# Adding the FFN result to the residual: VectorE adds replaced by accumulating transfers in three of four blocks, with a new instruction order

## The chip, the cores and the metric

The kernel runs on one core of one Trainium2 chip. The metric is the time of one execution on the device in microseconds (us). A core has five engines with a queue of instructions each: PE (TensorE, matmuls), ACT (ScalarE), DVE (VectorE), POOL (GpSimd) and SP (SyncE, which here only issues transfers). Each takes its instructions strictly in the order in which they were written, and waits on semaphores for the others. Transfers run on 16 DMA engines. SBUF is the on-chip memory with 128 partitions, PSUM the memory into which TensorE writes.

## What is computed

Two layers stand one behind the other on a sequence of 2048 tokens with 640 features, in bfloat16: a long convolution with gating (its convolution over 2048 tokens is written with an FFT), then a gated FFN with 1728 hidden features. Each has a layer norm ahead of it and a residual around it.

```python
def _A_ref(q, k, v, shift_k, ssm_k, ssm_D):
    ...
        k_shift = k_shift + k_pad[:, t:t + S, :] * shift_k[:, ks - 1 - t][None, None, :]
    kv = k_shift * v
    ...
    y_f = kv_f * kf_f[None, :, :, :]
    y = irfft2(y_f)[:, 0, :S, :]
    y = y + kv * ssm_D[None, None, :]
    return q * y

def _B_ref(x, w_gate, w_up, w_down):
    g = _silu(x @ w_gate)
    u = x @ w_up
    return (g * u) @ w_down

x = A_q
h = x + _A_ref(_layernorm(x), A_k, A_v, A_shift_k, A_ssm_k, A_ssm_D)
h2 = h + _B_ref(_layernorm(h), B_w_gate, B_w_up, B_w_down)
```

The last line is the one that matters here: the FFN result is added to h.

## The kernel before

The 2048 tokens are handled in four blocks (0 to 3) of 512. A block lies in SBUF as 128 partitions with four tokens each; one of the four columns of tokens (j = 0 to 3) is a tile of 128 x 640.

**What a block does.** `xload` brings x into one of two buffers, xh0 (blocks 0 and 2; in lists of the order xh_72) or xh1 (blocks 1 and 3; xh_73). `ln1` takes its mean and variance (L793 and L796 on ACT), the power on POOL (L806) and normalizes (L815). `kv` loads k (kT, transposed on the way) and v (vt) and makes the short convolution. `xfwd` transforms the product: matmuls with a table (L584, in block 2 L622), evacuated by ACT into tiles X and FO. `prod` multiplies spectra on DVE (tiles T and Y, from the filter's spectra C). `inverse` goes back (L832), multiplies (L859), and makes the second layer norm of each column: ACT sums (L870, L872, L876), POOL takes a power (L883), ACT applies it (L886, L888), and SP transposes the result into hnT. The filter's spectra are made once at the start from kc (its four loads are kc_100 to kc_103).

**The FFN of a block** (`ffn`) is 14 gate-and-up tiles: ten matmuls of 128x512 each (L913 gate, L914 up; a 14th of five, L924, holds the rest of both). ACT evacuates each as a SiLU (gu, L936) and a copy (ub, L938, two buffers), and DVE multiplies them (L940). Then come four groups of 26 down matmuls (L956) into PSUM, one for each column j, with a pair (L968) that adds the 14th tile.

**The residual add**, which the change touches, has three forms. Which blocks use which is set by the tuples RD and RA. Before, RA = (0, 1, 2): ACT evacuates a down result into the SBUF buffer dn5 (tile dn, L976) and adds the mean that the first layer norm had taken away; DVE then adds dn to xh (L983). Block 3 has one DVE instruction for both (L986). Behind it SP writes xh to the output (L990).

**What hangs on it.** The x of block 2 is loaded into the buffer of block 0, and that of block 3 into the buffer of block 1. So the load waits for the four output transfers of the block before last, which wait for its four sums. SP takes its queue in order: whatever stands behind an output transfer waits with it.

**PSUM** has four units of 128 x 1024 float32. A gate-and-up tile, a transform tile or a down result takes one, from its first matmul until ACT or DVE has read it. TensorE can be four tiles ahead of ACT, not more.

**The order.** Each instruction (or group) is a task with a number; the table `ORDER` lists for every engine its tasks in the order in which they are written out. The function `schedule` follows the lists, assigns the PSUM units and puts a few filler matmuls (L249) where it reckons with a pause of TensorE; `emit` writes the instructions with their waits.

Of the kernel before, what the change touches and what calls it, by code (L numbers as in the profile page):

```python
# [58 lines left out]
class _Graph:  # L59
# [170 lines left out]
    def emit(self, block):  # L230
# [75 lines left out]

ORDER = {
    "pe": """
# [7 lines left out]
    """,  # L316
    "act": """
# [12 lines left out]
    """,  # L330
    "dve": """
# [10 lines left out]
    """,  # L342
    "pool": """
        5 6 10 11 8 7 9 151 202 195 209 205 216 198 212 219 134 336 135 421 403 394 412 529 610 628 601 619 736 822 813 840
        831
    """,
    "sp": """
# [3 lines left out]
    """,  # L351
}

# [1 line left out]
def bass_sequential_preLN__ssm_conv_h3__swiglu_ffn__prompt_kernel(  # L355
# [38 lines left out]
    with ExitStack() as es:  # L394
# [67 lines left out]
        epc = sb("epc", o + 544, [4], f32)  # L462
        assert o + 576 <= SBB + 16481 - A0, o + 576

        BN, DIRECT, D8, PT, BN2, ST, R4, PAIR, WARM, ACC, EA, KD, RD, LA, RA = (0,), (), (), (0,), (), (0,), ('xf2',), True, 24, (), True, (2, 3), (), (1, 2, 3), (0, 1, 2)
        g = _Graph(nc, es)

        def cpe(n, k):
# [601 lines left out]
```

## Time and profile before

| | us |
|---|---|
| median of 3 runs | 269.81 |
| lowest and highest | 269.46, 269.82 |
| the profiled execution, its own time | 269.68 |
| its span, first to last instruction | 267.8 |
| PE busy in the span | 254.6 |
| ACT busy | 206.8 |
| DVE busy | 201.7 |
| POOL busy | 28.7 |
| granted clock of TensorE | 0.998 |

The page of a profile gives for each engine its busy time, and for each group of instructions (line, engine, operation, tile written <- tiles read, shape, count) busy us, mean ns of one, and how long the engine stood idle just before them, with what ended that wait behind the arrow. Lines of the timeline begin with start and duration in us from the start of the span; in brackets the idle time before and its releaser. A row of the window view gives a stretch and the busy us in it. Matmuls overlap each other, so the duration of one is longer than the distance to the next.

### The profile page before, as it was taken

The page shows a single profiled execution, that of the slowest core. Times are in us where ns is not written, and L with a number is a line of the kernel's source. Part 1 is how long each engine was busy: PE and PEld are TensorE (multiplying, and loading weights), DVE is VectorE, ACT ScalarE, POOL GpSimd, SP SyncE. Part 2 cuts the span into 40 slices and gives each one's busy share as a digit, 9 for nine tenths or more (in the row PEclk, how much of TensorE's full clock was granted, in tenths as well). Part 3 has the DMA queues.
Part 4 walks back from the last instruction along what each step waited for, and adds up shares of the span by engine and source line. Part 5 has one row for each costly group of instructions (what it writes and reads, how often), then busy time and mean ns, then how long its engine had stood idle before and what let it go on. Part 6 is the DMA issues. An engine that isn't in the chain of part 4 may idle for free.

```text
span 267.8 us, 4162 instructions
## 1 busy us (share of the span) xinstructions
PE 254.6 (95%) x1635; PEld 140.1 (52%) x1635; DVE 201.7 (75%) x282; ACT 206.8 (77%) x394; POOL 28.7 (11%) x37
## 2 busy tenths in 40 slices
PE   7899898999999998899899999999999989999995
PEld 5466563445445655444346567544446654444563
DVE  1599999999999998899999999999994000042204
ACT  2799999989887979948989997689799965346400
POOL 1000306011140042000040202000200200000000
PEclk9999999999999999999999999999999999999999
DMA  6999809959755637452000445500000150010004
GB/s 171 345 351 379 316 16 257 143 119 321 137 94 102 103 77 147 98 183 88 2 0 3 100 83 137 174 0 1 0 2 0 19 82 0 0 51 0 0 2 148
DMA packets 43557, 28.47 MB, mean 106 GB/s; under 512 B 32273, under 2 KB 41234, under 8 KB 43538
## 3 DMA queue, kind: packets, MB, share of 16 engines
q1 hardware_dynamic: 41824, 25.58, 35.4%
q0 software_dynamic: 1056, 2.62, 5.4%
q8 instruction: 13, 0.21, 0.3%
q10 hardware_dynamic: 658, 0.01, 0.1%
q14 instruction: 6, 0.05, 0.1%
HBM read 15.69 MB, written 2.62 MB: 68 GB/s over the span
## 4 chain that ended last, share of the span: by engine, by line
PE 41%; ACT 32%; DVE 15%; DMA 5%; SPq 2%; issue 2%; POOL 1%; ACTq 0%; DVEq 0%
PE ps L913 13%; PE ps L914 13%; PE ps L956 8%; PE ps L584 5%; ACT xh L815 4%; ACT ub L938 3%; ACT qo L856 3%; DMA vt<-in_A_v_dram 3%; DVE T L755 3%; ACT qo L872 3%; ACT qo L870 2%; DVE T L761 2%; ACT KT L545 2%; ACT gu L936 2%; DVE gu L940 2%; ACT qo L888 2%
## 5 line engine op out<-in xcount | busy, mean ns | idle before, releaser
L956 PE MATMUL ps<-Wd,gu 128*128 128x384 bf16 (+1 forms) x416 | 59.1, 300 | 0.1
L913 PE MATMUL ps<-hnT,GA 128*128 128x512 bf16 x140 | 53.1, 379 | 1.2 <-DMA hnT<-qo 0.7
L914 PE MATMUL ps<-hnT,UA 128*128 128x512 bf16 x140 | 53.1, 379 | 0.0
L956 PEld LDWEIGHTS ps<-Wd,gu 128*128 128x128 bf16 x416 | 39.9, 98 | 18.1 <-issue 1.6
L913 PE MATMUL ps<-hnT,GB 128*128 128x512 bf16 x120 | 45.5, 379 | 0.7 <-ACT gu L936 0.7
L914 PE MATMUL ps<-hnT,UB 128*128 128x512 bf16 x120 | 45.5, 379 | 0.0
L936 ACT ACTIVATE gu<-ps 128x512 bf16<-128x512 f32 x52 | 30.6, 598 | 17.8 <-PE ps L914 17.6
L938 ACT ACTIVATE ub<-ps 128x512 bf16<-128x512 f32 (+1 forms) x60 | 33.1, 566 | 6.6 <-PE ps L914 3.4
L940 DVE TENSOR_TENSOR gu<-gu,ub 128x512 bf16<-128x512 bf16 x52 | 21.0, 419 | 22.2 <-ACT ub L938 19.6
L755 DVE TENSOR_TENSOR T<-X,C 128x2560 bf16<-128x2560 bf16 x20 | 29.7, 1486 | 0.3
L756 DVE TENSOR_TENSOR T<-X,C 128x2560 bf16<-128x2560 bf16 x20 | 29.7, 1485 | 0.1
L913 PEld LDWEIGHTS ps<-hnT,GA 128*128 128x128 bf16 x140 | 13.7, 98 | 18.1 <-DMA hnT<-qo 1.0
L883 POOL TENSOR_TENSOR mv<-mv,half 128x1 f32<-128x1 f32 x16 | 15.3, 965 | 70.7 <-ACT mv L876 70.7
L584 PE MATMUL ps<-KT,ftab 128*128 128x320 bf16 x128 | 20.5, 301 | 2.0 <-DMA ftab<-cst_ftab 0.9
L914 PEld LDWEIGHTS ps<-hnT,UA 128*128 128x128 bf16 x140 | 13.7, 98 | 15.5
L913 PEld LDWEIGHTS ps<-hnT,GB 128*128 128x128 bf16 x120 | 11.7, 98 | 15.5 <-ACT gu L936 1.7
L761 DVE TENSOR_TENSOR T<-T 128x1280 bf16<-128x1280 bf16 x24 | 19.3, 819 | 0.2
L914 PEld LDWEIGHTS ps<-hnT,UB 128*128 128x128 bf16 x120 | 11.7, 98 | 13.8
L806 POOL TENSOR_TENSOR st<-st,half 128x8 f32<-128x8 f32 x4 | 9.1, 2267 | 91.2 <-ACT st L800 91.2
L771 DVE TENSOR_TENSOR Y<-Y,T 128x2560 bf16<-128x2560 bf16 x12 | 17.8, 1485 | 0.1
L584 PEld LDWEIGHTS ps<-KT,ftab 128*128 128x128 bf16 x128 | 10.3, 97 | 10.7 <-DMA ftab<-cst_ftab 1.4
L815 ACT ACTIVATE xh<-xh,st 128x640 bf16<-128x640 bf16 x16 | 14.5, 933 | 1.6 <-DVE st L808 1.6
(94 smaller groups left out, 372.8 us busy)
## 6 DMA issues: line engine op xcount, KB each, us to landing
kc<-in_A_ssm_k_dram SPq DMA_DIRECT2D x4, 640.0 KB, 9.2
xh<-in_A_q_dram SPq DMA_DIRECT2D x4, 640.0 KB, 4.2
vt<-in_A_v_dram SPq DMA_DIRECT2D x4, 640.0 KB, 6.3
out_dram<-xh SPq DMA_DIRECT2D x16, 160.0 KB, 1.9
Wd<-in_B_w_down_dram SPq DMA_DIRECT2D x1, 1280.0 KB, 6.5
C<-C POOLq DMA_DIRECT2D x1, 1280.0 KB, 13.6
C<-R POOLq DMA_DIRECT2D x1, 1280.0 KB, 9.4
UA<-in_B_w_up_dram SPq DMA_DIRECT2D x1, 1120.0 KB, 9.1
```

Source lines behind the costliest of these rows:

```text
L584: last = e.matmul(pt.f(c, W), ftab[:, cs, j, f * P:(f + 1) * P], src[:, j, c * W:(c + 1) * W], start=(j == par), stop=(j == par + 2))
L755: g.add("dve", nm, lambda e, x=x, k=k, t1=t1: e.tensor_tensor(out=t1, in0=x, in1=k, op=ALU.mult), cdve(2560), r=[x, k], w=[t1])
L756: g.add("dve", nm, lambda e, x=x, k=ksw, t2=t2: e.tensor_tensor(out=t2, in0=x, in1=k, op=ALU.mult), cdve(2560), r=[x, k], w=[t2])
L761: g.add("dve", nm, lambda e, p=p, q=q, d=d, op=op: e.tensor_tensor(out=d, in0=p, in1=q, op=op), cdve(1280), r=[p, q], w=[d])
L771: g.add("dve", nm, lambda e, y=y, z=z: e.tensor_tensor(out=y, in0=y, in1=z, op=ALU.add), cdve(2560), r=[y, z], w=[y])
L815: g.add("act", nm, lambda e, j=j, xj=xj: e.activation(out=xj, in_=xj, func=ACTF.Identity, scale=s[:, 4, j:j + 1], bias=s[:, 5, j:j + 1]), ...
L913: e.matmul(pt.f(0, N), wg[:, c, f0:f0 + P], hnT[:, c, :], start=(c == 0), stop=(c == NC5 - 1))
L914: last = e.matmul(pt.f(1, N), wu[:, c, f0:f0 + P], hnT[:, c, :], start=(c == 0), stop=(c == NC5 - 1))
L936: g.add("act", nm, lambda e, pt=pt, gv=gv, a=ps_g, ts=ts: e.activation(out=gv, in_=pt.f(a[0], N, a[1])[:, ts], func=ACTF.Silu, scale=gain) ...
L938: g.add("act", nm, lambda e, pt=pt, uv=uv, a=ps_u, ts=ts: e.activation(out=uv, in_=pt.f(a[0], N, a[1])[:, ts], func=ACTF.Copy, scale=gain) ...
L940: g.add("dve", nm, lambda e, uv=uv, gv=gv: e.tensor_tensor(out=gv, in0=gv, in1=uv, op=ALU.mult), cdve(n), r=[gv, uv], w=[gv])
L956: last = e.matmul(pt.flat(c1 - c0, P + c0), slots[fb][:, j * P:(j + 1) * P], Wd[:, fb, c0:c1], start=(fb == 0 and not second), stop=(fb == ...
```

## The change

The tuples change places: RD = (0, 1, 2) and RA = (). In blocks 0 to 2 ACT evacuates as before, and the sum is made by a transfer that POOL issues and that adds its source to what its destination holds. The destination is one column of xh (1280 bytes in each partition), the source a column of dn5, which lies there as five runs of 128 elements (256 bytes) in each partition. Twelve DVE additions of 128 x 640 go away, twelve transfers of 160 KB come. Nothing changes in block 3.

```diff
-        BN, ..., RD, LA, RA = (0,), ..., (), (1, 2, 3), (0, 1, 2)
+        BN, ..., RD, LA, RA = (0,), ..., (0, 1, 2), (1, 2, 3), ()
```

The code that the tuples choose between is the same in both:

```python
if i in RD:
    g.add("pool", nm, lambda e, x=x, z=z: e.dma_start(x.rearrange("p (c n) -> p c n", c=NC5), z, accum_op=ALU.add), 1100,
          r=[z, x], w=[x], dma=(1200, 0), lat=1700, lock=False)
else:
    g.add("dve", nm, lambda e, x5=x.rearrange("p (c n) -> p c n", c=NC5), z=z: e.tensor_tensor(out=x5, in0=x5, in1=z, op=ALU.add),
          cdve(D), r=[z, x], w=[x])
```

All five lists of `ORDER` are new, so that nearly every stretch of the program stands in another order. Line numbers of the changed kernel are smaller by one behind the table, which has a line less. One row of each list:

```diff
-        5 6 10 11 8 7 9 151 202 195 209 205 216 198 212 219 134 336 135 421 403 394 412 529 610 628 601 619 736 822 813 840
-        831
+        8 10 6 7 5 11 9 151 202 195 216 205 209 198 219 212 134 336 135 421 403 295 412 394 299 304 308 529 610 601 488 628
+        619 497 501 492 736 822 840 813 831 699 695 708 704
...
-        17 0 18 136 3 19 62 227 57 67 223 224 222 4 310 312 230 311 226 231 225 207 200 214 221 319 323 320 316 315 228 229
+        17 0 18 136 3 62 19 310 67 57 222 4 224 225 312 223 311 207 230 200 221 214 320 316 319 226 315 323 228 229 227 231
```

The first place is POOL's queue from the filter's combination (tile C) to the powers of block 2 (tile mv is the statistics of one column of the second layer norm, st those of the first). Before:

```order
L664 DMA C_51<-R_53 128x4x1280
L883 TENSOR_TENSOR mv_122<-mv_122,half 128x1
L883 TENSOR_TENSOR mv_120<-mv_120,half 128x1
L883 TENSOR_TENSOR mv_119<-mv_119,half 128x1
L883 TENSOR_TENSOR mv_121<-mv_121,half 128x1
L806 TENSOR_TENSOR st_0_117<-st_0_117,half 128x8
```

and in the change:

```order
L663 DMA C_51<-R_53 128x4x1280
L882 TENSOR_TENSOR mv_122<-mv_122,half 128x1
L882 TENSOR_TENSOR mv_120<-mv_120,half 128x1
L979 DMA xh_72<-dn_94 128x5x128
L882 TENSOR_TENSOR mv_121<-mv_121,half 128x1
L882 TENSOR_TENSOR mv_119<-mv_119,half 128x1
L979 DMA xh_72<-dn_94 128x5x128 x3
L805 TENSOR_TENSOR st_0_117<-st_0_117,half 128x8
```

The first transfer of block 0 stands between two powers of block 1, the other three behind the last. Block 1's stand the same way in block 2; block 2's four stand at the end of the queue.

The second place is ACT's queue behind the last evacuation of block 0's FFN (the row just ahead is one L976 before, and two in a row, L975 x2, in the change), up to the first statistics of block 2's x (L793; X_56 and FO are the transform of block 2, gu and ub the first FFN tiles of block 1). Before:

```order
L628 ACTIVATE FO<-ps 128x640 x4
L628 ACTIVATE X_56<-ps 128x640 x2
L938 ACTIVATE ub_79<-ps 128x512
L628 ACTIVATE X_56<-ps 128x640 x2
L936 ACTIVATE gu_81<-ps 128x512
L938 ACTIVATE ub_78<-ps 128x512
L793 ACTIVATE qo_77,st_0_117<-xh_72 128x640
```

and in the change:

```order
L627 ACTIVATE X_56<-ps 128x640
L627 ACTIVATE FO<-ps 128x640
L627 ACTIVATE X_56<-ps 128x640
L627 ACTIVATE FO<-ps 128x640 x2
L627 ACTIVATE X_56<-ps 128x640 x2
L937 ACTIVATE ub_78<-ps 128x512
L937 ACTIVATE ub_79<-ps 128x512
L935 ACTIVATE gu_84<-ps 128x512
L935 ACTIVATE gu_82<-ps 128x512
L935 ACTIVATE gu_81<-ps 128x512
L937 ACTIVATE ub_79<-ps 128x512
L792 ACTIVATE qo_77,st_0_117<-xh_72 128x640
```

L793 (now L792) stands behind six FFN rows from three tiles instead of three rows from two.

The third place is SP's queue at the start of the program. Before:

```order
L481 DMA ftab<-cst_ftab 128x2048
L481 DMA vt<-in_A_v_dram 128x2560
L481 DMA kc_102<-in_A_ssm_k_dram 128x5x512
L481 DMA PK<-in_B_w_up_dram 128x5x64
L481 DMA kc_101<-in_A_ssm_k_dram 128x5x512
L481 DMA kc_103<-in_A_ssm_k_dram 128x5x512
L481 DMA UA<-in_B_w_up_dram 128x5x896
```

and in the change:

```order
L480 DMA ftab<-cst_ftab 128x2048
L480 DMA kc_102<-in_A_ssm_k_dram 128x5x512
L480 DMA vt<-in_A_v_dram 128x2560
L480 DMA xh_73<-in_A_q_dram 128x2560
L480 DMA kc_103<-in_A_ssm_k_dram 128x5x512
L480 DMA kc_101<-in_A_ssm_k_dram 128x5x512
L480 DMA GA<-in_B_w_gate_dram 128x5x896
```

The load of v for block 0 stands behind a load of the filter instead of ahead of it. The rows keep the names of the kernel before in the text that follows.

More of the change, by code (lines that the diff above doesn't have):

```diff
@@ L463, in bass_sequential_preLN__ssm_conv_h3__swiglu_ffn__prompt_kernel @@
         assert o + 576 <= SBB + 16481 - A0, o + 576
-        BN, DIRECT, D8, PT, BN2, ST, R4, PAIR, WARM, ACC, EA, KD, RD, LA, RA = (0,), (), (), (0,), (), (0,), ('xf2',), True, 24, (), True, (2, 3), (), (1, 2, 3), (0, 1, 2)
+        BN, DIRECT, D8, PT, BN2, ST, R4, PAIR, WARM, ACC, EA, KD, RD, LA, RA = (0,), (), (), (0,), (), (0,), ('xf2',), True, 24, (), True, (2, 3), (0, 1, 2), (1, 2, 3), ()
         g = _Graph(nc, es)
```

61 rows, old and new, of the table ORDER are left out of this document.

## The prediction

> **What bounds the kernel now.** I read the page's first part, then the busy time of long stretches, then who waited for whom, and last the timeline at the two places where the residual add meets other work. The page first (engine, busy us, share, instructions):
>
> ```profile
> PE 254.6 (95%) x1635; PEld 140.1 (52%) x1635; DVE 201.7 (75%) x282; ACT 206.8 (77%) x394; POOL 28.7 (11%) x37
> ```
>
> Three stretches of the window view (stretch, its length, then busy us of PE, PEld, DVE, ACT, POOL, the granted clock, the DMA share, GB/s):
>
> ```profile
> 52.11:264.60 212.49, 208.55 (x1237) 111.97 (x1236) 158.77 (x219) 161.97 (x324) 21.16 (x17) 1.00 0.30 71
> 15.00:203.00 188.00, 182.15 (x1161) 98.19 (x1159) 182.86 (x241) 167.33 (x319) 25.69 (x22) 1.00 0.48 119
> 203.00:268.00 65.00, 60.64 (x366) 33.93 (x364) 12.93 (x28) 31.51 (x67) 2.28 (x4) 0.99 0.12 31
> ```
>
> From the first FFN matmul (52.11) to the last down matmul TensorE lacks only 212.49 - 208.55 = 3.9 us, at full clock. That is the most a change behind 52 us can win. VectorE is just as full until 203 us (182.86 of 188) and nearly idle after. So VectorE time counts up to 203 us, but only through TensorE's pauses. Their causes between 52 and 264.6 us (who waited, for whom, us in total, times, longest):
>
> ```profile
> PE ps L968 <- ACT kT L717: 1.1, 1, 1.1
> PE ps L913 <- ACT gu L936: 0.7, 2, 0.6
> PE ps L913 <- DMA hnT<-qo: 0.7, 1, 0.7
> PE ps L913 <- ACT FO L628: 0.5, 1, 0.5
> PE ps L693 <- ACT qo L856: 0.2, 1, 0.2
> PE ps L622 <- ACT FO L628: 0.2, 1, 0.2
> PE ps L968 <- DVE gz L940: 0.2, 1, 0.2
> ```
>
> Together 3.6 us, almost all on ScalarE.
>
> **What is removed.** Twelve VectorE adds and the wait ahead of one of them:
>
> ```profile
> L983 DVE TENSOR_TENSOR xh<-xh,dn 128x640 bf16<-128x640 bf16 x12 | 5.6, 486 | 11.9 <-ACT dn L976 11.8
> 102.53 0.49 DVE L983 TENSOR_TENSOR xh<-xh,dn 128x640 bf16<-128x640 bf16 x1 [1.29 <-ACT dn L976]
> ```
>
> 12 x 0.486 = 5.8 us. Block 2's four fall behind 203 us and are worth nothing. The eight of blocks 0 and 1 are 3.9 us, plus the 1.29 us in which VectorE stood at 102 us: 5.2 us in the stretch where it is full. ScalarE's evacuations (dn) stay as they are.
>
> **What is added.** Twelve accumulating transfers on POOL's queue, 160 KB each, in runs of 256 bytes: 128 x 5 = 640 packets. The trace has the same kind of transfer twice, at 1280 KB in 512 packets of 2560 bytes; the fourth row is the queues part for 77 to 84 us, when only one of them moved, the fifth that for 212 to 219.9 us, when only transposes in 256-byte packets did:
>
> ```profile
> 59.49 1.49 POOL L664 DMA_DIRECT2D C<-C  x1 [12.42 <-DVE C L554]
> 75.14 1.31 POOL L664 DMA_DIRECT2D C<-R  x1
> C<-R POOLq DMA_DIRECT2D x1, 1280.0 KB, 9.4
> q0 software_dynamic: 517, 1.31, 107.3%
> q1 hardware_dynamic: 2688, 0.66, 51.0%
> ```
>
> POOL's issue took 1.4 us for 512 packets, so I put 640 at 1.75 us. An accumulating packet took 1.073 x 16 x 7000 / 517 = 232 ns; a plain one of 256 bytes 0.51 x 16 x 7900 / 2688 = 24 ns. From issue to landing 9.4 us, of which about 7.0 moved data: 2.4 us are fixed. No row has accumulating packets of 256 bytes. By bytes they cost 232 / 10 = 23 ns, per packet 232 ns; each of 16 engines gets 40, so 0.9 to 9.3 us. I take 50 ns, twice the plain packet, hence 2.0 us: the 24 ns row has the same size, and adding reads two operands. Issue to landing is then 2.4 + 0.35 (longer issue) + 2.0 = 4.75 us, between 3.3 and 12.
>
> What lies behind an issue on POOL: one transfer of block 0 stands among the powers of block 1's layer norm, one of block 1 among those of block 2; the others follow the last power. ScalarE's L886 waits for each power. Between the request of the power behind the issue and its L886, ScalarE has two long rows, an L888 and an L870 or an L717 and an L872, some 1.6 us, and the request itself comes about 1.5 us after the issue starts, so 1.75 us and a power of 0.72 are covered. If that cover were gone, ScalarE would stand as it does once now:
>
> ```profile
> L888 ACT ACTIVATE qo<-xh,mv 128x640 bf16<-128x640 bf16 x12 | 10.9, 913 | 0.1
> L872 ACT ACTIVATE qo<-xh,mv 128x640 bf16<-128x640 bf16 x12 | 9.9, 823 | 0.1
> L883 POOL TENSOR_TENSOR mv<-mv,half x16: 544/720/3342, 42.5 to 214.5; 128x1 f32<-128x1 f32 x16
> 100.85 0.29 ACT L886 ACTIVATE mv<-mv 128x1 f32<-128x1 f32 x1 [1.79 <-POOL mv L883]
> ```
>
> 1.79 us there, which became TensorE's 1.1.
>
> **What is late next.** The out transfers wait for the sums, the load of the x that reuses the buffer waits for the out transfers, and ScalarE's L793 stands in order for that x. Blocks 0 to 2, then 1 to 3:
>
> ```profile
> 109.52 0.79 ACT L976 ACTIVATE dn<-ps,st 128x640 bf16<-128x640 f32 x1
> 114.33 1.32 SPq L990 DMA_DIRECT2D out_dram<-xh  x3
> 117.13 0.34 SPq L481 DMA_DIRECT2D xh<-in_A_q_dram  x1
> 112.54 0.38 PE L913 MATMUL ps<-hnT,GA 128*128 128x512 bf16 x1 [0.49 <-ACT FO L628]
> 114.48 0.38 PE L914 MATMUL ps<-hnT,UA 128*128 128x512 bf16 x1
> 117.59 0.60 ACT L936 ACTIVATE gu<-ps 128x512 bf16<-128x512 f32 x1 [0.86 <-PE ps L914]
> 121.09 0.74 ACT L793 ACTIVATE qo<-xh 128x640 bf16<-128x640 bf16 x1 [2.41 <-DMA xh<-in_A_q_dram]
> 128.90 0.39 PE L913 MATMUL ps<-hnT,GB 128*128 128x512 bf16 x1 [0.55 <-ACT gu L936]
> 131.39 0.39 PE L913 MATMUL ps<-hnT,GB 128*128 128x512 bf16 x1 [0.16 <-ACT gu L936]
> 166.07 0.79 ACT L976 ACTIVATE dn<-ps,st 128x640 bf16<-128x640 f32 x1 [0.79 <-PE ps L956]
> 174.55 0.74 ACT L793 ACTIVATE qo<-xh 128x640 bf16<-128x640 bf16 x1 [1.96 <-DMA xh<-in_A_q_dram]
> 120.00:140.00 20.00, 19.29 (x89) 8.42 (x88) 19.80 (x27) 16.98 (x37) 2.96 (x1) 1.00 0.10 40
> 170.00:185.00 15.00, 15.00 (x74) 7.13 (x73) 14.90 (x18) 11.10 (x24) 0.00 (x0) 1.00 0.14 46
> ```
>
> Call D the end of the last dn: 110.31 and 166.86. Now x is used at D + 10.8 and D + 7.7. In the change the third transfer is issued at D - 0.7 (two dn in a row, one lasting 0.79), the fourth at D + 1.05, and lands at D + 5.8. From the last out's issue (114.33 + 2 x 0.44) to the x load 1.9 us, from there to L793 4.0 (121.09 - 117.13): x is there at D + 11.7, that is 122.0 and 178.6: 0.9 and 4.0 us later than now. But L793 has been moved too. In block 2 it now follows the third gate-and-up tile instead of the second. A tile is ten matmuls; the first and the tenth start 1.94 us apart, so a tile takes 2.16 us, and the third ends at 117.59 + 2.16 = 119.75. Four ScalarE rows follow, at about 0.5 us (121.09 - 2.41 - 117.59 = 1.09 for two): L793's turn comes at 121.7. In block 3 it moves from behind the first tile to behind the third. Its turn was at 174.55 - 1.96 = 172.6; two tiles (4.3 us) and two transform pieces of four matmuls come on top (about 0.55 each: from the end of the tenth matmul, 114.86, to 117.59, less a tile): 178. So ScalarE's 2.41 and 1.96 us shrink to a few tenths. TensorE's two pauses at 128.90 and 131.39 hang on the first: -0.7 us. The second has none behind it.
>
> **The order elsewhere.** The pauses between 100 and 113 us (1.1, 0.2 and 0.5) meet a new order in which the pair matmuls stand ahead of the convolution's and one transform piece ahead of the last down group. Their bounds are all gone (-1.8) and a new pause as long as the longest (+1.1); VectorE's freed 5.2 us serve this stretch, so I take -0.4. The remaining 1.1 us (0.2 + 0.2 + 0.7) I leave.
>
> At the front the load of kc_102 (640 KB) now goes ahead of the first vt (a row of the chain of waits, two of the timeline, the GB/s of the 40 slices, one ScalarE stretch):
>
> ```profile
> 7.29 7.57 DMA vt<-in_A_v_dram
> 14.96 1.23 DVE L713 TENSOR_TENSOR vt<-ps,vt 128x1024 bf16<-128x1024 f32 x1 [0.26 <-PE ps L584]
> 16.10 1.01 DVE L786 BATCH_NORM_STATS2 bst<-xh 128x6 f32<-128x320 bf16 x2
> GB/s 171 345 351 379 316 16 257 143 119 321 137 94 102 103 77 147 98 183 88 2 0 3 100 83 137 174 0 1 0 2 0 19 82 0 0 51 0 0 2 148
> 20.00:25.00 5.00, 4.63 (x46) 3.20 (x43) 4.86 (x7) 5.00 (x8) 0.00 (x0) 1.00 1.06 379
> ```
>
> 655 KB at 360 GB/s is 1.8 us that vt and the VectorE chain behind it start later. 1.0 us of statistics is moved ahead of vt, so 0.8 us is left; ScalarE is full there (5.00 of 5) and has other filter rows to do meanwhile. Between 0 and 1.8 I take +0.4.
>
> **Sum.** -0.7 - 0.4 + 0.4 = -0.7 us. The profiled execution took 269.68 us (span 267.8 and 1.9 around it), 0.13 below the median of 269.81. 269.68 - 0.7 = 269.0; on the median 269.1.
>
> [...]
>
> **The rivals.**
>
> *The sums land late (slower).* If a packet of 256 bytes costs near the 232 ns of a large one, landing comes up to 7.3 us later. ScalarE has spare 20 - 16.98 = 3.0 us in 120 to 140 and 15 - 11.1 = 3.9 us in 170 to 185; the wait at L793 decides once it is longer. At half way (+3.65 us) L793 waits 3.9 and 4.2 us: 0.9 + 0.3 lost, and the gain of 0.7 with it: 269.8 + 1.2 = 271.0. At the full 7.3 us it waits 7.6 and 7.9: 4.6 + 4.0 lost, 278.4. Against it: the 24 ns row.
>
> [...]
>
> *The new order costs more than it gives (slower).* Front at its bound, 1.8 instead of 0.4, and pauses at 100 to 113 as now: -0.7 + 1.8 = +1.1: 270.9. For it: ScalarE is full up to 50 us and has no room to make up; against: the moved statistics.
>
> *VectorE's freed time reaches further (faster).* All pauses of 100 to 132 us go (-1.8 - 0.7) and the front costs nothing: 269.81 - 2.5 = 267.3; with the front at 0.4, 267.7. For it: VectorE is full to 203 us.
>
> *It does not show.* The adds are hidden, TensorE pauses elsewhere as long: 269.8.
>
> **How the numbers follow.** Forecast 0.42, its own range 268.2 to 270.1; further reach 0.12, new order 0.26, late landing 0.12, lock 0.04, nothing 0.04. About 0.2% (0.54 us) is what a measurement here can tell from no change, so faster means below 269.27. The forecast's band gives 0.25 faster, 0.15 the same, 0.02 slower; the new order 0.22 slower, 0.04 the same; further reach faster; landing and lock slower. Together 0.37 faster, 0.23 the same, 0.40 slower. The range 267.6 to 271.8 takes in further reach, the new order and half of the late landings.
>
> **What would show it.** Right: no L983 row; 12 more DMA issues on POOL of 1.5 to 2 us; a sum landed about 4.8 us after its issue; L793's waits for x below 1 us; no pause among the gate-and-up matmuls of block 1; first FFN matmul at 52 to 53 us. Wrong: landings over 8 us, L793 waiting over 3 us, powers queued behind an issue with L886 waiting, or a first FFN matmul beyond 53.5 us.

## The result

The change made the kernel slower by 0.32%: 270.47 us median of 20 runs (269.18 to 272.85) against 269.70 for the kernel before beside it (268.38 to 270.05), a ratio of 1.0032 with a 95% interval of 1.0016 to 1.0047. The forecast was 269.1 us, a little faster; the time lies inside the range that went with it (267.6 to 271.8), but on the other side of no change. The profiled execution took 270.92 us with a span of 269.0, against 269.68 and 267.8. Two executions of one kernel below, the old order with transfers, fell into a slower state of the chip; its median below is that of the other four (with all six it is 282.84, which later expectations quote).

### The profile after

The lines that answer to those quoted of before. From the page, the engines (busy us, share, instructions; 16 matmuls are missing from this trace, which has 1637 weight loads), the queue that carries POOL's transfers (packets, MB, share of 16 engines) and the new transfers (number, KB, us from issue to landing):

```profile
PE 253.9 (94%) x1621; PEld 142.2 (53%) x1637; DVE 197.6 (73%) x270; ACT 206.2 (77%) x394; POOL 45.3 (17%) x49
q0 software_dynamic: 8928, 4.59, 15.3%
xh<-dn POOLq DMA_DIRECT2D x12, 160.0 KB, 5.0
```

VectorE lost its 12 additions. The kernel with additions in the same order (below) has in its page:

```profile
q0 software_dynamic: 1056, 2.62, 5.6%
```

The transfers are what was forecast: 8928 - 1056 = 7872 packets took (15.3 - 5.6)% of 16 x 269 us, or 53 ns each (forecast 50), and a sum lands 5.0 us behind its issue (forecast 4.75).

TensorE's pauses behind 52 us, as in the view of who waited for whom (us in total, times, longest):

```profile
PE ps L621 <- DVE vt L725: 1.4, 1, 1.4
PE ps L912 <- ACT gu L935: 1.0, 2, 0.9
PE ps L912 <- ACT ub L937: 0.8, 2, 0.5
PE ps L913 <- ACT FO L596: 0.5, 1, 0.5
PE ps L913 <- DMA hnT<-qo: 0.4, 1, 0.4
PE ps L955 <- ACT kT L716: 0.4, 1, 0.4
PE ps L913 <- ACT FO L627: 0.4, 1, 0.4
PE ps L831 <- DVE IO L553: 0.3, 1, 0.3
```

They add up to 5.3 us where the kernel before had 3.6. Almost none of the old ones is left, and a new set has taken their place. The largest stands in these timeline rows (SP's and POOL's issues, VectorE, TensorE; in brackets the idle time before a row and what ended it):

```profile
96.79 6.79 SPq L485 DMA_TRANSPOSE kvo<-kT  x5
98.98 1.51 POOL L979 DMA_DIRECT2D xh<-dn  x1
104.53 0.96 DVE L725 TENSOR_TENSOR vt<-vt,kvo 128x1536 bf16<-128x1536 bf16 x1 [0.99 <-DMA kvo<-kT]
106.74 0.76 DVE L725 TENSOR_TENSOR vt<-vt,kvo 128x512 bf16<-128x512 bf16 x2 [1.25 <-DMA kvo<-kT]
107.56 0.45 PE L621 MATMUL ps<-vt,ftab 128*128 128x320 bf16 x2 [1.45 <-DVE vt L725]
```

Block 0's first sum is issued at 98.98, in the middle of the five transposes into kvo that block 2's vt waits for. The tile view of kvo in 94 to 109 us gives their time to landing (least, median, most):

```profile
DMA to landing us min/median/max: 2.4/3.9/4.6
```

The same view of the kernel with additions in the same order, where no sum moves, gives

```profile
DMA to landing us min/median/max: 2.4/2.5/2.5
```

So a transpose into kvo with no sum beside it landed in 2.4 to 2.5 us; those next to the sum took up to 4.6. The order places one transform piece of block 2 (L621) ahead of the last down group, so TensorE stands for it. In 102 to 104 us both queues move, each at about 60% of the engines' time (packets, MB, share):

```profile
q1 hardware_dynamic: 821, 0.20, 63.1%
q0 software_dynamic: 328, 0.08, 60.8%
```

One thing more moves there. The first queues row for 104 to 106 us in the change is a single packet of 16 KB on the queue that the view calls "instruction", 4.1% of 16 engines for 2 us, or 1.3 us on one engine; the second is that of the kernel with additions in 103 to 107 us, 1.5 us on one engine; the third is the landing of that kernel's transposes into hnT in 100 to 113 us:

```profile
q8 instruction: 1, 0.02, 4.1%
q8 instruction: 1, 0.02, 2.4%
DMA to landing us min/median/max: 2.6/3.5/5.0
```

The two transposes that go out beside this packet (103.29 and 104.61 us) take 5.0 and 4.3 us though no sum moves; the two behind them take 2.6 and 2.7. In the change the last transpose into kvo, issued at 102.28 behind two that the sum had held up, is still under way when this packet comes, and lands after 4.4 us. With the sum out of the way (first sum late, below) it lands in 2.5, about as the packet comes. So the sum starts the delay, and the packet may add to it; no run removes the packet.

Block 1's sums show the sharing without this packet. The transposes into hnT beside them land, with additions (155 to 172 us) and in the change (160 to 172), in

```profile
DMA to landing us min/median/max: 2.6/2.6/2.6
DMA to landing us min/median/max: 2.6/3.2/4.8
```

### The profile page after: what moved, and what is told of

The parts are those of the page before. It is cut to its first block, busy times and chain, and to the rows that moved or that the text cites. A ratio compares the mean times of both kernels' runs of the same rounds, so it can differ in the third digit from the quotient of the medians.

```text
span 269.0 us, 4149 instructions
## 1 busy us (share of the span) xinstructions
PE 253.9 (94%) x1621; PEld 142.2 (53%) x1637; DVE 197.6 (73%) x270; ACT 206.2 (77%) x394; POOL 45.3 (17%) x49
## 3 DMA queue, kind: packets, MB, share of 16 engines
q0 software_dynamic: 8928, 4.59, 15.3%
## 4 chain that ended last, share of the span: by engine, by line
PE 31%; ACT 27%; DVE 20%; DMA 16%; SPq 3%; issue 1%; POOL 1%; DVEq 0%
PE ps L913 9%; PE ps L912 9%; PE ps L955 5%; DMA xh<-dn 4%; DVE T L755 4%; ACT qo L887 3%; ACT qo L871 3%; DMA xh<-in_A_q_dram 3%; ACT qo L869 3%; DVE T L754 3%; DMA kvo<-kT 3%; PE ps L583 3%; ACT qo L855 2%; DVE Y L760 2%; DVE X L553 2%; ACT ub L937 2%
## 5 line engine op out<-in xcount | busy, mean ns | idle before, releaser
L912 PE MATMUL ps<-hnT,GA 128*128 128x512 bf16 x132 | 50.0, 379 | 0.9 <-ACT gu L935 0.9
L937 ACT ACTIVATE ub<-ps 128x512 bf16<-128x512 f32 (+1 forms) x60 | 33.9, 572 | 18.3 <-PE ps L913 11.1
L912 PE MATMUL ps<-hnT,GB 128*128 128x512 bf16 x117 | 44.4, 379 | 1.0 <-ACT ub L937 0.8
L882 POOL TENSOR_TENSOR mv<-mv,half 128x1 f32<-128x1 f32 x16 | 14.3, 901 | 61.7 <-ACT mv L875 61.7
L979 POOL DMA_DIRECT2D xh<-dn x12 | 18.3, 2049 | 13.8 <-ACT dn L975 13.8
L912 PEld LDWEIGHTS ps<-hnT,GB 128*128 128x128 bf16 x120 | 11.7, 98 | 16.1 <-ACT ub L937 1.6
L805 POOL TENSOR_TENSOR st<-st,half 128x8 f32<-128x8 f32 x4 | 7.6, 1892 | 70.2 <-ACT st L799 70.2
L583 PEld LDWEIGHTS ps<-KT,ftab 128*128 128x128 bf16 x128 | 11.2, 98 | 10.4 <-ACT KT L544 2.0
```

The lines of the kernel that those rows point to most:

```text
L583: last = e.matmul(pt.f(c, W), ftab[:, cs, j, f * P:(f + 1) * P], src[:, j, c * W:(c + 1) * W], start=(j == par), stop=(j == par + 2))
L912: e.matmul(pt.f(0, N), wg[:, c, f0:f0 + P], hnT[:, c, :], start=(c == 0), stop=(c == NC5 - 1))
L937: g.add("act", nm, lambda e, pt=pt, uv=uv, a=ps_u, ts=ts: e.activation(out=uv, in_=pt.f(a[0], N, a[1])[:, ts], func=ACTF.Copy, scale=gain) ...
L979: g.add("pool", nm, lambda e, x=x, z=z: e.dma_start(x.rearrange("p (c n) -> p c n", c=NC5), z, accum_op=ALU.add), 1100, r=[z, x], w=[x], d ...
```

## The experiments

Every kernel was timed beside the kernel before on the same chip. In all of them the planner sets no filler matmuls behind 60 us (before and the change have none there either). Some have a line or more in addition, so line numbers move; the names stay. "Pauses" is the sum of TensorE's pauses behind 52 us that the timeline shows in its profiled execution. It is a rough measure: matmuls of 379 ns start 216 ns apart, so a start that is up to 0.16 us late shows no idle time.

| kernel | median us | before | ratio, 95% interval | pauses us |
|---|---|---|---|---|
| before | 269.70 | | | 3.6 |
| the change | 270.47 | 269.70 | 1.0032 (1.0016 to 1.0047) | 5.3 |
| new order, additions | 270.86 | 270.28 | 1.0027 (1.0009 to 1.0045) | 3.6 |
| old order, transfers | 281.28 | 270.28 | 1.0412 (1.0363 to 1.0460) | 10.9 |
| first sum late | 270.55 | 270.28 | 1.0007 (0.9987 to 1.0027) | 3.6 |
| sums in landing order | 273.87 | 270.28 | 1.0115 (1.0075 to 1.0155) | 5.6 |
| the same, wide runs from elsewhere (FFN result left out) | 268.75 | 269.92 | 0.9954 (0.9933 to 0.9975) | 2.6 |
| old order in the first 86 us | 270.22 | 269.92 | 1.0009 (0.9992 to 1.0026) | 4.2 |
| block 1 on VectorE | 270.00 | 269.92 | 1.0013 (0.9989 to 1.0037) | 2.3 |
| both of these | 270.29 | 269.92 | 1.0016 (1.0000 to 1.0031) | 3.9 |
| **the change, wide runs** | **267.35** | 269.87 | **0.9922 (0.9892 to 0.9953)** | 1.2 |
| landing order, wide runs | 268.38 | 269.87 | 0.9954 (0.9937 to 0.9970) | 2.1 |
| old order, transfers, wide runs | 280.42 | 269.87 | 1.0399 (1.0364 to 1.0435) | 9.9 |
| before, layout alone | 270.19 | 269.87 | 1.0020 (1.0001 to 1.0039) | 4.0 |
| old order, outputs back, wide | 273.59 | 269.93 | 1.0139 (1.0094 to 1.0184) | 7.5 |
| old order, outputs back, small | 279.29 | 269.93 | 1.0344 (1.0272 to 1.0417) | 11.2 |

### The new order with additions

```diff
-RD, LA, RA = (0, 1, 2), (1, 2, 3), ()
+RD, LA, RA = (), (1, 2, 3), (0, 1, 2)
-pool: ... 403 295 412 394 299 304 308 529 ... 601 488 628 619 497 501 492 ... 831 699 695 708 704
+pool: ... 403 412 394 529 ... 601 628 619 ... 831
+dve:  ... 569 295 ... 571 304 ... 572 299 308 ... 773 488 ... 726 497 ... 780 492 ... 778 501 ... 827 695 708 704 699
```

> The changed kernel's order with the twelve sums back on VectorE (each put behind the VectorE instruction that runs when its dn is ready; nothing else is moved; POOL carries powers alone). Theory A, the transfers cost: TensorE's pause of 1.45 us for vt at 107.6 shrinks below 0.5, because nothing shares the queues with the transposes into kvo at 101 to 104 us; x of blocks 2 and 3 is there 3 us earlier or more, L792 no longer waits, and the pause of 0.86 us at 183 goes: 270.9 - 2.0 = 268.9, less what 3.9 us of VectorE take back. Theory B, the new order costs by itself: the pauses at 75 to 85 us (1.0) and at 143 to 172 us (1.25) stay, VectorE's 3.9 us come on top, and the time is that of the changed kernel, 270.5, or above.

Measured 270.86 us, 1.0027: not to be told from the change. Neither theory holds alone. The pause for vt is gone, as A said, and L792 (here L793) no longer waits at 124 us and 0.34 us at 179. But other pauses came, the largest because VectorE is late with the inverse transform's input:

```profile
143.74 2.35 PE L832 MATMUL ps<-IO,itab 128*128 128x320 bf16 x16 [1.07 <-DVE IO L554]
```

The listed pauses add up to 3.6 us, as before, but the span is 269.0 us: 0.3 us of the difference lie ahead of the first FFN matmul (52.45) and 0.9 in late matmul starts that the list does not count. So it seems that in this order taking 12 additions off VectorE does help, and that something in the transfers takes the same amount back; the wide runs below bear it out.

### The old order with transfers

```diff
-RD, LA, RA = (), (1, 2, 3), (0, 1, 2)
+RD, LA, RA = (0, 1, 2), (1, 2, 3), ()
-dve:  (the twelve tasks)
+pool: ... 394 295 412 304 299 308 ... 628 488 601 619 497 492 501 ... 831 708 695 699 704
```

> The order of before with the twelve sums as transfers on POOL (each behind the power that precedes its dn, the late ones behind the last power of the next block; nothing else is moved). Theory A, the transfers cost: the fourth sum of block 0 lands about 5.8 us behind the last dn, x of block 2 is there at 123 us and that of block 3 at 179 instead of 121.1 and 174.5, L793 waits 4.2 and 6.4 us instead of 2.4 and 2.0, and TensorE's pauses behind them grow by 1.8 and about 2: 0.5 to 3 us above before. Theory B, the transfers are innocent and the new order costs: VectorE's 5.2 us come free, 269.7 or up to 0.7 below.

Measured 281.28 us, 11 above before where at most 3 were expected. TensorE stood 8.6 us for hnT, the transposed input of the next FFN. SP and POOL in block 1:

```profile
165.28 5.42 SPq L989 DMA_DIRECT2D out_dram<-xh  x2
166.16 3.04 POOL L979 DMA_DIRECT2D xh<-dn  x2
170.75 4.92 SPq L485 DMA_TRANSPOSE hnT<-qo  x3
```

In the old order two outputs of block 1 stand ahead of three transposes into hnT. With additions these outputs were ready at 162.5; now SP stands at them until the sums have landed, and the transposes go out at 170.75 instead of 163.6; 2.3 us of this are the lateness that the kernel has by then (its transposes into kvo start at 156.93 instead of 154.67).

### The first sum late

```diff
-pool: ... 421 403 295 412 394 299 304 308 ...
+pool: ... 421 403 412 394 295 299 304 308 ...
```

> The changed kernel with one task moved on POOL: the first sum of block 0 goes behind the last two powers of block 1 instead of ahead of them, so it is issued at about 106 us instead of 99. Theory A, this transfer's packets share the queues with the transposes into kvo: these land in about 2.5 to 3.5 us instead of 3.9 to 4.6, VectorE has vt 1 us earlier and TensorE's pause of 1.45 us at 107.6 falls to 0.5 or below: 0.3 to 1.0 us faster than the changed kernel. Theory B, the transposes are late by their place in the queue alone: the pause stays above 1.2 us and the time does not change.

Measured 1.0007, some 0.25% below the change, though the two intervals overlap. The mechanism is as theory A has it: the transposes into kvo land in

```profile
DMA to landing us min/median/max: 2.4/2.5/2.6
```

and the pause for vt is gone. Two others stand in its place. The first sum, issued at 106.97 instead, now meets the last two transposes into hnT, which take 4.7 and 3.7 us to land (with additions 2.7 and 2.6), and TensorE waits 0.71 us for them at 113. At 183 it waits 1.19 for gu, where L792 has waited 1.96 for x.

### Sums in landing order

```diff
-pool: ... 394 299 304 308 ... 619 497 501 492 ...
+pool: ... 394 304 299 308 ... 619 497 492 501 ...
-sp: ... 309 300 296 305 503 ... 502 489 493 498 710 ...
+sp: ... 296 305 300 309 503 ... 489 498 493 502 710 ...
```

> The changed kernel with the sums on POOL, and the output transfers on SP, in the order in which their dn are ready (block 0: third column ahead of the second; the output that lands last goes last, not first; block 1 the same). Theory A, x comes late because sums and outputs stand in the wrong order: x of block 2 is there at about 123 instead of 125.6 us and that of block 3 at 179 instead of 180.9, L792's waits of 1.40 and 1.62 us go, and TensorE's pause of 0.86 us at 183 with them: 0.5 to 0.9 us faster than the changed kernel. Theory B, x does not set the end: the pause at 183 us stays or moves, and the time stays within 0.2 us.

Measured 273.87 us: the order that should have brought x earlier cost 3.4 us more. The third sum of block 1, issued at 165.9 us instead of 168, now moves while the transposes into hnT move. POOL's issues and TensorE's first FFN matmul, from the timeline, and the time to landing of the four transposes, from the tile view of hnT:

```profile
164.44 3.05 POOL L979 DMA_DIRECT2D xh<-dn  x2 [0.77 <-ACT dn L975]
173.15 0.61 PE L912 MATMUL ps<-hnT,GA 128*128 128x512 bf16 x1 [2.83 <-DMA hnT<-qo]
DMA to landing us min/median/max: 2.6/3.8/6.3
```

And x of block 3 did not come earlier: the last two sums of block 1 take 7.2 and 7.6 us to land instead of 4.2 to 5.7, and its load is issued at 177.21 us instead of 176.96. The matmul behind the pause took 0.61 us instead of 0.38 (last section).

### The same with wide runs from elsewhere

```diff
-e.dma_start(x.rearrange("p (c n) -> p c n", c=NC5), z, accum_op=ALU.add)
+e.dma_start(x, GA[:, 0, 0:D], accum_op=ALU.add, max_dma_last_dim=2560)
```

> The kernel of the sums in landing order (273.9 us, TensorE's pause of 2.83 us for hnT at 173), but each sum takes its source from one run of 1280 bytes in each partition instead of five of 256: 128 packets in place of 640. For that it adds a stretch of the gate weights instead of the FFN's result; it still waits for dn, so the instants are those of the transfer. Theory A, the many small packets hold up the transposes into hnT: these land in 2.6 to 3.5 us instead of 4.8 to 6.3, the sums in 3 to 4 instead of 5 to 7.6, the pause falls below 0.7 and the time to 270 to 271. Theory B, the adding of the 160 KB itself holds the queues, whatever the packets: landings and pause stay, 273 to 274.

The source is a stretch of the gate weights, so this kernel leaves the FFN result out; it serves for its time alone. Measured 268.75 us, 5.1 below the kernel with small packets, and 0.46% below before. Transposes, queues, order and bytes are the same; the run length of the source changed, and with it its place, which a later experiment (landing order, wide runs) sets right. Sums land in 3.7 us, the pause for vt is gone and that for hnT is 0.91. Theory A holds, beyond its number.

### Old order in the first 86 us; block 1 on VectorE; both

```diff
 (first sum late, and)
+all five lists: tasks that the planner starts before 86 us in the old kernel, in the old order, then the rest in the new
```

> The kernel with the first sum late (270.55), but every instruction that the planner starts in the first 86 us stands in the order of before; the rest in the new order, with the sums as transfers. Theory A, the new order itself costs in the gate-and-up tiles of block 0 (pauses for ub of 0.26 and 0.34 us at 78 and 85 us, and a first FFN matmul that is no earlier): these pauses go, 0.4 to 0.7 us faster than the first sum late, and so below before. Theory B, ScalarE only hands its backlog on: the same time, 270.3 to 270.8.

```diff
 (first sum late, and)
-RD, LA, RA = (0, 1, 2), (1, 2, 3), ()
+RD, LA, RA = (0, 2), (1, 2, 3), (1,)
-pool: ... 488 ... 497 501 492 ...
+dve:  ... 773 488 ... 726 497 ... 780 492 ... 778 501 ...
```

> The kernel with the first sum late (270.55), but the four sums of block 1 are VectorE additions again, where they stood in the experiment with the new order and additions. Theory A, the transfers of block 1 share the queues with the transposes into hnT of block 2 and make x of block 3 late: the pauses at 170 us (0.23 for hnT) and at 183 us (1.19 for gu) fall to 0.7 in sum, and the time is 0.3 to 0.8 us lower, at that of before or below. Theory B, VectorE's 1.9 us cost as much there: no change.

> Both edits together: the order of before in the first 86 us, then the new order with the first sum late, and block 1's sums on VectorE; blocks 0 and 2 keep transfers. Theory A: the two gains add, 0.7 to 1.5 us below the first sum late, so some 0.5 to 1.2 us below before. Theory B: the time stays at that of before within 0.3 us.

None of the three is told apart from the first sum late (1.0009, 1.0013 and 1.0016 against 1.0007). The pauses for ub at 78 and 85 us did go with the old front, but a wait of 1.10 us for gz at 94 us came where the two orders meet. With block 1 on VectorE the pauses at 170 and 183 us (1.42 in sum) fell to 0.64, as theory A says, and the time did not follow. Its profiled execution had a pause of 3.06 us for kT at 48.8 us that no other shows, so its pauses can't be compared. The two do not add. With small pieces, mixing the forms brought nothing that can be told from noise.

### The change with wide runs

dn5 overlays the last five of the 13 product tiles (gu): the result of a column may only go where that column's own products, already used, have stood. These are five pieces of 256 bytes. If the five tiles lie between each other, the same bytes are one run of 1280. In the cut, `_Five` is a small class that returns the pieces of one such tile; left out are the lines by which ScalarE's SiLU and VectorE's product write a tile in four pieces.

```diff
-dn5 = sb("dn5", o + 8192, [NC5, N])
+dn5 = sb("dn5", o + 8192, [4, NC5, P])
+gu[8:13] = [_Five(dn5, k) for k in range(NC5)]   # tile 8 + k is dn5[:, :, k, :]: four groups of 128, 640 apart
-z = dn5[:, :, P * j:P * j + P]
+z = dn5[:, j]
-e.dma_start(x.rearrange("p (c n) -> p c n", c=NC5), z, accum_op=ALU.add)
+e.dma_start(x, z.rearrange("p c n -> p (c n)"), accum_op=ALU.add, max_dma_last_dim=2560)
```

> The changed kernel in its own order, with the last five product tiles of the FFN laid out so that a column of dn5 is one run: tile 8 + k holds its four groups of 128 columns 640 elements apart, and the five tiles lie between each other. The result of a column then overlays what its own down matmuls have read, as before, but in one run of 1280 bytes: 128 packets for each sum instead of 640. It computes the same. Theory A, the small packets were the cost: a sum lands in 3.7 us instead of 5.0, the transposes into kvo and hnT in 2.6 to 3.2, the pause for vt (1.45 us) falls to 0.3 or less, x comes 1 to 1.5 us earlier, and the time is 1.0 to 1.8 us below the changed kernel, 0.1 to 1.0 below before. Theory B, the new order costs by itself: 0.2% or more above before, as with additions in this order (1.0027).

Measured 267.35 us, 0.9922: 0.8% below before and 3.1 us below the change; theory A expected 1.0 to 1.8. This version beats both. The queue, the sums' landing, all of TensorE's pauses behind 52 us, and POOL's three last issues of block 0:

```profile
q0 software_dynamic: 2784, 4.59, 10.8%
xh<-dn POOLq DMA_DIRECT2D x12, 160.0 KB, 3.4
PE ps L925 <- ACT ub L953: 0.6, 2, 0.3
PE ps L925 <- DMA hnT<-qo: 0.3, 1, 0.3
PE ps L971 <- ACT kT L729: 0.3, 1, 0.3
109.61 2.65 POOL L995 DMA_DIRECT2D xh<-dn  x3 [3.12 <-ACT dn L991]
```

Against the change, in the same order, these have gone: vt 1.45, FO 0.37 and 0.52, IO 0.33, gu 0.86 and 0.19 us; with what came off ub, kT and hnT the list is 4.2 us shorter. The first FFN matmul starts 0.35 us later (52.36), and the spans differ by 3.7 (269.0 and 265.3). That the small pieces cost these pauses is shown; by which way each of them came (transposes, a later x, POOL's issues) is shown for vt alone, by the first sum late. An issue costs POOL 0.88 us instead of 1.52. A packet takes (10.8 - 5.6)% x 16 x 265.3 / 1728 = 128 ns, so the 160 KB of a sum occupy the 16 engines 18 us in all (144 packets) instead of 35 (656). In both, 16 packets of a sum are not pieces of it, which are 128 and 640.

### Landing order, old order and layout alone

```diff
 (the wide layout, in the landing order; in the old order; and in the kernel before with its additions)
```

> The same layout with the sums and outputs in landing order, the kernel that took 273.9 us with small packets. Theory A: as with the stretch of gate weights, 268.8 us, 0.4% below before, and 0.3 us or more faster than the wide layout in the order of the change, since x of block 3 comes 2 us earlier. Theory B, that gain came from the source lying elsewhere, not from its runs: 270 or above.

> The same layout in the order of before, with the twelve sums as transfers, the kernel that took 282.8 us with small packets. Theory A, nearly all of the 12.6 us came from small packets ahead of the transposes into hnT: the waits for hnT (2.3 and 5.7 us) fall below 1 us each, the clock stays at 1.0, and the time comes to 269 to 272 us. Theory B, the old order leaves the transfers no place whatever their packets: 275 us or more.

> The kernel before, with its additions on VectorE and its own order, and only the layout of the last five product tiles and of dn5 changed. Both theories: the layout by itself does nothing, 1.000 within 0.2%; ScalarE's SiLU and VectorE's product on those tiles take 0.60 and 0.43 us as now. Should it be faster by 0.3% or more, the gain of the wide kernels is the layout's and not the packets'.

Landing order: 268.38, as with the source elsewhere, so the gain is the runs'. But its median is 1.0 us above the change's own order, against what I expected (the two intervals just overlap): the third sum still meets the transposes, and TensorE waits 1.06 us for hnT. Layout alone: 1.0020, nothing or a little worse, so the layout does not explain the gain. The old order with wide runs: 280.42, theory B. There the packets alone decide little (0.9 us); hnT is awaited 7.8 us.

### The old order with three outputs moved back

```diff
-sp: ... 397 296 406 415 ... 723 489 498 631 604 622 502 493 ...
+sp: ... 397 406 415 296 ... 723 631 604 622 489 498 502 493 ...
```

> The order of before with the sums as transfers in wide runs (280.4 us), and three outputs moved on SP: the first of block 0 and the first two of block 1 now stand behind the last transpose into hnT of the next block. Theory A, SP's queue held the transposes: those of block 1's sums are issued at about 166 us instead of 172.5, the pause of 3.72 us for hnT falls below 1.5, the clock stays at 1.0 behind it, and the time falls by 5 us or more, to 275 or less. Theory B, the queues are shared whatever SP does: the pause stays above 3 us and the time above 278.

> The same move with small packets (282.8 us before it). Theory A, queue and packets both count: the pause of 5.70 us falls to 2 to 3.5, and the time to 276 to 279, 2 us or more above the wide one. Theory B, the queue alone counts: within 1 us of the wide one.

Measured 273.59 (wide) and 279.29 (small). With small packets the move is worth 2.0 us, and the ranges of the two kernels overlap (277.14 to 281.27 and 280.01 to 283.42); with wide ones it is worth 6.8. Wide packets alone gave 0.9, with the move 5.7: the two together take off 7.7 of the 11.0 us, and neither much alone. Block 1's transposes, in the wide kernel, are issued at once:

```profile
165.18 4.90 SPq L498 DMA_TRANSPOSE hnT<-qo  x3
172.67 0.38 PE L926 MATMUL ps<-hnT,UA 128*128 128x512 bf16 x1 [0.94 <-DMA hnT<-qo]
```

With small packets the pause at that place is 3.62, and the transposes land in up to 6.6 us (wide 4.6). Theory A, queue and packets both, holds in both runs, though the clock did not stay at 1.0 in the wide one (0.51 in 114.6 to 118 us, last section). Where the wide kernel's last 1.4% above before come from stays open; its largest pauses are 2.16 us at 114.7, for ScalarE's evacuation of block 2's transform, and 1.31 at 183.

## Why the prediction was wrong, step by step

**What bounds the kernel**: right in the main. From the change to its version with wide runs the list of TensorE's pauses is 4.2 us shorter and the span 3.7. But the list is not the whole measure, as the new order with additions showed (3.6 us of pauses in spans of 267.8 and 269.0). Of the 3.6 us of before, 2.7 were on ScalarE, not almost all.

**What is removed**: sized too low, not too high. The forecast gave VectorE's 5.2 us a part of -0.4. Where the transfers do little harm (wide runs), the change's order is about 1% (2.8 us) faster with them than with additions (0.9922 against 1.0027). The rival "freed time reaches further", at 267.3 us, tells what the mechanism is worth: with wide runs no pause is listed between 100 and 132 us, and the median is 267.35.

**What is added**: each number was near (issue 1.52 us, forecast 1.75; packet 53 ns, forecast 50; landing 5.0, forecast 4.75), and this is nevertheless **the step that failed**. The sum charged the 2.0 us of moving to the sums alone: the prediction followed the landing of dn into outputs and x, and asked of no other transfer what it does meanwhile; what the others lose stood in the sum at nothing. The transposes into kvo and hnT, which TensorE awaits, move in the same microseconds. Into kvo they went from 2.5 to 4.6 us (a packet of the queue "instruction" may have part in the last of them), into hnT from 2.6 to 4.8, in the sums in landing order to 6.3. With pieces five times as long, in the same order and with the same bytes, the change is 3.1 us faster. That the packet came near 50 ns was in part luck: the reason given, that adding reads two operands, was not tested. The trace shows the sharing: in 102 to 104 us two queues move at once, at 63.1% and 60.8% of the engines' time, and the transposes are slower.

**What is late next**: the chain from the last dn to x was put at 11.7 us and took 13.2 in both blocks (112.36 to 125.59 and 167.74 to 180.94). The last issue, the landing and the last output, for block 2 and its wait:

```profile
110.85 4.56 POOL L979 DMA_DIRECT2D xh<-dn  x3 [4.79 <-ACT dn L975]
118.44 1.82 SPq L989 DMA_DIRECT2D out_dram<-xh  x4
121.75 0.34 SPq L480 DMA_DIRECT2D xh<-in_A_q_dram  x1
125.59 0.74 ACT L792 ACTIVATE qo<-xh 128x640 bf16<-128x640 bf16 x1 [1.40 <-DMA xh<-in_A_q_dram]
180.94 0.74 ACT L792 ACTIVATE qo<-xh 128x640 bf16<-128x640 bf16 x1 [1.62 <-DMA xh<-in_A_q_dram]
```

The sum landed 6.1 us behind the dn (forecast 5.8). But SP has the output of the last sum first in its list, so the other three are issued behind it, 1.4 us that were not in the chain. And the last dn itself, which the prediction took where it ended in the kernel before, ended 2.05 us later in block 0, behind the pause for vt, and 0.9 later in block 1. The waits are 1.40 and 1.62 us where a few tenths were forecast. The first costs nothing: the two pauses of 0.7 us are gone, as forecast. Behind the second, which "has none behind it", there is now a pause of 0.86 us for gu at 183, on another tile. The wait is not all of it: with additions in this order it is 0.65 behind a wait of 0.34. Net +0.15 instead of -0.7.

**The order elsewhere**: -0.4 was forecast for 100 to 113 us; it is 0.0. The 1.77 us of before gave way to 1.45 for vt and 0.37 for FO, and the 1.45 is the sharing above (gone in the first sum late and with wide runs). What VectorE gained there it spent waiting for kvo. New pauses in other stretches were priced at nothing: 0.19, 0.48 and 0.33 in block 0's tiles, 0.33, 0.40 and 0.52 later, less 0.68 of old ones gone: +1.6 us. The wide kernel shows what of them is the order's own (0.58 for ub, 0.29 for kT) and what came with small packets (the rest).

**The front**: +0.4 was forecast. The first FFN matmul starts at 52.0 us, before at 52.1; over the other profiles it lies at 52.2 to 52.9 in the new order (but for the one with the pause at 48.8) and at 52.3 to 52.9 in the old one. Nothing.

Sum: -0.7 became +0.15, -0.4 became 0, +0.4 became -0.1, and 0 became +1.6: +1.65, where the spans of the two profiled executions say +1.2 (what is below 0.15 us is in no list) and the medians +0.77.

**The rivals.** "The new order costs more than it gives" has the nearest time (270.9) and half of the reason: the pauses at 100 to 113 are as large as before, but not the front. "The sums land late" failed on its condition: they land as forecast, and others land late. "Lock" in the chances (0.04), a busy VectorE that holds up the issue, is shown by no run: in the change an issue took 1.51 to 1.53 us in the stretches of the first eight, where VectorE was busy 12.6 of 12.7 us, and 1.54 us in that of the last four (223.7 to 230 us), where it stood idle. The cover of the issue among the powers held: L885 waits for POOL once, 0.75 us, before 1.79. Of the signs of being wrong none came; of those of being right "L793's waits for x below 1 us" failed, and a pause of 0.37 us is left at the start of block 1's tiles. None of the signs watched the transposes. The chances gave slower the largest share, 0.40, while the forecast time was on the faster side.

## What to carry to other kernels

Work that is moved from an engine to a transfer can be paid for by the transfers beside it, as here (transposes into kvo landed in up to 4.6 us instead of 2.5): before counting on it, list what else is in flight in those microseconds and who waits for it, and keep the pieces long, since one layout change that made 256-byte pieces 1280 bytes turned +0.3% into -0.8%. A result that lands later also blocks what is queued behind its consumer on the in-order queue of transfers (in the old order three transposes into hnT went out at 170.75 us instead of 163.6, 2.3 us of it older lateness): outputs go behind loads and transposes that the next stage needs (three outputs moved back were worth 2.0 us with small pieces, 6.8 with long ones). And two parts of a change can each look worthless alone: in the old order the transfers cost 4%, with additions the new order cost 0.3%, and only together, with long pieces, did they win.

## What the runs showed of the hardware

**Small pieces inside SBUF.** A packet of an accumulating transfer took the engines 53 ns with pieces of 256 bytes and 128 ns with pieces of 1280, averaged with the 16 packets of a sum that are not pieces; if those took nothing, it would be 54 and 144. So five times the bytes took 2.4 to 2.6 times the time. With the 232 ns that the prediction found for 2560 bytes, an estimate is some 35 ns for a packet and 0.08 ns for a byte.

**The clock behind a pause.** Behind TensorE's pause of 2.83 us in the sums in landing order the granted clock was halved for 3 us (windows: length, then busy us of PE, PEld, DVE, ACT, POOL, the clock, the DMA share, GB/s):

```profile
173.00:176.00 3.00, 2.85 (x7) 1.05 (x8) 3.00 (x3) 0.00 (x0) 0.00 (x0) 0.50 0.65 169
176.00:179.00 3.00, 3.00 (x16) 1.48 (x15) 2.96 (x4) 1.19 (x2) 0.00 (x0) 0.98 0.41 108
```

That costs about 1.5 us on top of the pause, an estimate: half of the 3 us at a clock of 0.50. The one execution of this kernel whose mean clock stayed at 1.0 took 270.97 us, the other five (0.987 to 0.994) 273.4 to 274.5. Pauses of 1.82, 2.14, 2.16, 3.60, 3.72 and 5.70 us in the old-order kernels, and that of 3.06 us at 48.8, did the same (0.50 to 0.54 in windows of 2.5 to 4 us behind them; behind the one of 1.82, matmuls of 0.63 us instead of 0.38 from 115.03 to 118.00 us); one of 2.31 and one of 3.62 did not (1.00 in the windows behind them), and the pauses of up to 1.45 us in the change never did (1.00). A pause of 3.62 us without the lower clock and one of 1.82 with it show that here the length alone does not decide. What decides is not settled by these runs.
